# Routed mixture-of-experts kernel: low parts of the weights on VectorE alone while the routing runs, issued one by one; weights of the first expert split during its gather

## The chip, the core and the metric

The kernel runs on one core of a Trainium2 chip. Five engines take part, each with its own queue that is worked off in order: TensorE (PE, the matmuls; PEld is its loading of weights), VectorE (DVE), ScalarE (ACT), GpSimd (POOL) and SyncE (SP), which issues most DMA transfers. The metric is the device time of one execution in microseconds.

## The reference

Three layers follow each other, all in fp32. First comes attention with a local or a strided mask over 4 x 576 tokens, 8 heads of 64 columns; its output is a matrix x of 2304 tokens by 512. Then a routed layer of eight experts, with a greedy assignment by capacity:

```python
logits = x @ w_gate                       # 2304 x 8
order = np.argsort(-logits.flatten())     # best first
# each token goes to one expert, each expert takes cap = 2304 // 8 = 288 tokens
for e in range(8):
    h = np.maximum(x[assigned == e] @ w1[e], 0.0)      # 512 -> 1024
    out[assigned == e] = h @ w2[e]                     # 1024 -> 512
```

Last comes a dense layer of four experts over all tokens, out = sum over e of p[:, e] * (relu(y @ v1[e]) @ v2[e]), where p are given probabilities, each row divided by its sum.

## The kernel before

**Matmuls in three products.** A matmul of the two expert layers is made of three, so that it keeps nearly fp32 accuracy: each operand is split into a high part (a copy rounded to the type fp32r) and a low part (the operand minus its high part), and high x high, low x high and high x low are summed in PSUM. The high part is made by ScalarE. For activations the low part is made by VectorE straight from PSUM (`split`, L804: `xl`, `hl`, `y256l`, `y512l`). For weights the low part `wl` is `raw - wh`, with both inputs in SBUF.

**Units, steps, chunks.** `experts` (L703) runs 20 units: a unit "m1" g is routed expert g for its 288 tokens, a unit "m2" is one dense expert for one to three blocks of 256 or 512 tokens. The routed experts come at units 0, 3, 5, 7, 9, 11, 13, 15, and dense work on tokens already done lies between them. A unit has a step for each eighth of the hidden width and each block. A step is layer one, `l1` (12 matmuls into a PSUM tile `h`), and, two steps later (LK = 2), layer two, `l2` (into tiles `o`); between them the ReLU makes `hh` on ScalarE (L806) and `hl` on VectorE. A chunk is the weights of one eighth: two tiles `raw` of 128 x 512 (256 KB each, one DMA each, L770 and L771 on SP's queue), the high parts `wh` (two copies on ScalarE, L795) and the low parts `wl` (two subtractions, L801). There are 8 buffers for `raw`, which is four chunks, and 8 chunks of `wh` and `wl`.

**What sets the order of the weights' work.** `preps` (L991), called after each `l1`, makes the high parts of a chunk LA = 3 steps ahead of its first use (`prep_hi`, L788), and the low parts one step later (`prep_lo`, L797), both halves of a chunk in one go. `prep_lo` chooses the engine: all lows of odd chunks and the second half of even ones go to GpSimd, the first half of even chunks to VectorE. After the lows of a chunk `loads` (L773) issues the transfers of later chunks; a transfer into a `raw` buffer has to wait until both the high and the low of the chunk that lay in it are done.

**The routing.** Two generators run beside the matmuls. `chain_a` (L814) finds, for each expert, the threshold that lets 288 tokens through: a search in six rounds (`search`), where VectorE compares (`G`), TensorE counts by small matmuls (`pa`, L561), VectorE reduces the counts (`need`, `junk`), TensorE spreads the result (`pa`, L568) and VectorE forms the next thresholds (`d`, `th`, `kb`, `jk`). `chain_b` (L822) turns the found tokens into indices (`place`: `O`, `W`, matmuls L654 and L661, `idx`), gathers their rows by three indirect DMAs on GpSimd (`xg`, L833), transposes them (L850, for the first expert L857) and splits them into `xh` and `xl`. Each generator yields after a piece of work, and says when it wants to go on.

**The planner.** The order is written while the program is built. `Pace` (L676) keeps an estimated clock of TensorE (`nc.pe`, advanced by `mm`, L909, by each large matmul) and one of VectorE (`nc.dve`, advanced by 0.075 us + elements / 960 for each VectorE instruction). `tick` (L895) steps a generator when the time that it asked for (`wake`, L893) is reached. So small matmuls and VectorE work of the routing are put between large matmuls at places that depend on these estimates, and all five engines then work off fixed orders. The engine orders matter because a waiting instruction holds up everything behind it on its engine.

**The start.** When the search for expert 0 is done, L1005 to L1009 issue the loads of chunks 0 to 2, run the chains until the first gather is issued, prepare chunk 0 (`preps(0, 1)`), run on until the gathered rows are split (`x`), and prepare the next chunks. On SP's queue the small transfer `side<-xg` (L837), which waits for the gather, stands between the loads of chunk 2 and of chunk 3.

## Time and profile before

| what | value |
|---|---|
| median of 3 runs | 1290.42 us (1290.1 to 1298.86) |
| the profiled execution, its own time | 1290.25 us |
| its span, first to last instruction | 1288.5 us |
| mean granted TensorE clock | 0.968 |
| PE busy | 1226.5 us (95%) |
| DVE, ACT, POOL busy | 555.8, 417.7, 423.6 us |

The attention fills the time up to about 170 us, with the search for expert 0 at its end. The first routed expert's matmuls begin at 180.2 us. The searches for the other experts run beside the matmuls until shortly before 500 us, the gathers until some 700 us. From 830 us on only dense work is left. All times below are counted from the span's start. A busy PE is not PE at its peak: matmuls overlap, and at a lower granted clock they are longer and still count as busy.

### The profile page before, as it was taken

What the parts mean: (1) busy time and instruction counts of PE and PEld (TensorE: products, weight loads), DVE (VectorE), ACT (ScalarE), POOL (GpSimd) and SP (SyncE); (2) the same over time, 40 slices, a digit from 0 to 9 for tenths busy, and PEclk for the clock granted to TensorE, in tenths of its full rate; (3) what the DMA queues carried; (4) which work ended last, traced back from release to release, by engine and by line L of the source; (5) the groups of instructions that cost most, each with busy time, mean ns of one, the idle gap of its engine ahead of it and who ended that gap; (6) DMA issues with size and microseconds to landing.
All of it is one profiled execution on the core that took longest, in us unless ns stands there. A gap on an engine that the chain in (4) does not pass through costs nothing.

```text
span 1288.5 us, 21205 instructions
## 1 busy us (share of the span) xinstructions
PE 1226.5 (95%) x7883; PEld 1034.2 (80%) x7883; DVE 555.8 (43%) x1618; ACT 417.7 (32%) x1110; POOL 423.6 (33%) x385
## 2 busy tenths in 40 slices
PE   7899859888998999999999999999999999999997
PEld 5676658777877889889888898988888888888886
DVE  4476566978777663233134332422231122123212
ACT  4687543332332234134134252321130131013110
POOL 3133144645244355145155453620050022004101
PEclk7699979999999999999999999999999999999999
DMA  6664274544334345035134353520040021002001
GB/s 136 144 153 87 57 214 123 155 134 121 88 101 116 86 123 157 23 105 155 44 115 123 110 155 93 170 66 1 1 131 1 1 74 57 1 1 66 25 9 50
DMA packets 159767, 114.99 MB, mean 89 GB/s; under 512 B 45104, under 2 KB 136256, under 8 KB 159088
## 3 DMA queue, kind: packets, MB, share of 16 engines
q1 hardware_dynamic: 156592, 104.01, 29.2%
q0 software_dynamic: 3072, 9.62, 2.4%
q8 instruction: 62, 1.02, 0.3%
q14 instruction: 41, 0.34, 0.1%
HBM read 104.02 MB, written 9.58 MB: 88 GB/s over the span
## 4 chain that ended last, share of the span: by engine, by line
PE 81%; DVE 8%; DMA 3%; issue 3%; SPq 2%; ACT 1%; POOL 1%; POOLq 0%; DVEq 0%; ACTq 0%
PE h L910 37%; PE o L910 35%; DVE G L699 2%; DMA ks<-in_k_dram 2%; DVE wl L699 1%; DMA raw<-in_moe_w_dram 1%; PE pt L211 1%; PE pa L561 1%; PE tr L143 1%; SPq L67 1%; SPq L57 1%; PE xr L302 1%; DVE th L699 1%; PE av L224 1%; PE xr L305 1%
## 5 line engine op out<-in xcount | busy, mean ns | idle before, releaser
L801 POOL TENSOR_TENSOR wl<-raw,wh 128x512 fp32r<-128x512 f32 x239 | 336.4, 1424 | 571.8 <-ACT wh L795 481.3
L699 DVE SCALAR_TENSOR_TENSOR hl<-h,hh 128x256 fp32r<-128x256 f32 (+2 forms) x256 | 136.1, 532 | 588.8 <-ACT hh L806 585.5
L806 ACT ACTIVATE hh<-h 128x256 fp32r<-128x256 f32 (+2 forms) x256 | 120.8, 472 | 763.5 <-PE h L910 747.0
L910 PE MATMUL o<-wh,hl 128*128 128x512 f32 x576 | 229.9, 399 | 0.0
L910 PE MATMUL o<-wl,hh 128*128 128x512 f32 x576 | 229.3, 398 | 0.0
L910 PE MATMUL o<-wh,hh 128*128 128x512 f32 x576 | 228.7, 397 | 0.0
L795 ACT CAST wh<-raw 128x512 fp32r<-128x512 f32 x320 | 181.4, 618 | 9.5 <-DMA raw<-in_moe_w_dram 9.4
L910 PE MATMUL h<-hold,wh 128*128 128x512 f32 x384 | 152.4, 397 | 0.0
L910 PE MATMUL h<-y512l,wh 128*128 128x512 f32 x384 | 151.6, 395 | 0.0
L910 PE MATMUL h<-hold,wl 128*128 128x512 f32 x384 | 150.8, 393 | 0.0
L910 PEld LDWEIGHTS o<-wh,hl 128*128 128x128 f32 x576 | 108.7, 189 | 25.2 <-issue 0.3
L910 PEld LDWEIGHTS o<-wl,hh 128*128 128x128 f32 x576 | 108.8, 189 | 21.5
L910 PEld LDWEIGHTS o<-wh,hh 128*128 128x128 f32 x576 | 108.4, 188 | 21.8 <-issue 0.2
L910 PE MATMUL h<-y256h,wh 128*128 128x256 f32 x384 | 110.1, 287 | 0.0
L910 PE MATMUL h<-y256h,wl 128*128 128x256 f32 x384 | 109.9, 286 | 0.0
L910 PE MATMUL h<-y256l,wh 128*128 128x256 f32 x384 | 109.6, 285 | 0.0
L699 DVE TENSOR_TENSOR wl<-raw,wh 128x512 fp32r<-128x512 f32 x81 | 90.0, 1111 | 1.4 <-ACT wh L795 1.4
L910 PEld LDWEIGHTS h<-hold,wl 128*128 128x128 f32 x384 | 72.1, 188 | 17.6
L910 PEld LDWEIGHTS h<-hold,wh 128*128 128x128 f32 x384 | 72.1, 188 | 16.1
L910 PEld LDWEIGHTS h<-y512l,wh 128*128 128x128 f32 x384 | 72.1, 188 | 15.9
L910 PE MATMUL o<-hh,wh 128*128 128x288 f32 x256 | 77.2, 301 | 3.4 <-DVE acc L699 3.4
L910 PE MATMUL h<-xl,wh 128*128 128x288 f32 x256 | 78.9, 308 | 0.0
(221 smaller groups left out, 1838.1 us busy)
## 6 DMA issues: line engine op xcount, KB each, us to landing
raw<-in_moe_w_dram SPq DMA_DIRECT2D x320, 256.0 KB
vl<-in_v_dram SPq DMA_DIRECT2D x32, 96.0 KB
qs<-in_q_dram SPq DMA_DIRECT2D x4, 576.0 KB
ks<-in_k_dram SPq DMA_DIRECT2D x4, 576.0 KB
ql<-in_q_dram SPq DMA_DIRECT2D x16, 144.0 KB
kl<-in_k_dram SPq DMA_DIRECT2D x16, 144.0 KB
xd<-y512l SPq DMA_DIRECT2D x9, 192.0 KB
xd<-y512l SPq DMA_DIRECT2D x2, 576.0 KB
```

What stands on the lines that cost most here:

```text
L57: nc.sync.dma_start(T[nm][:, :, h, :], dap(src, (b * H + h) * hs, [6 * D, 96], [D, 6], [1, D]))
L67: nc.sync.dma_start(T["vs"][18 * p:18 * (p + m), t], dap(v, (b * H + 4 + h) * hs + 2 * rp * D, [2 * D, m], [32 * D, 18], [1, 2 * D]))
L143: nc.tensor.transpose(p[:, 72 * a:72 * a + 72], src[:, r:r + 2, :].rearrange("p r d -> p (r d)"), ident[:72, :72])
L211: nc.tensor.transpose(p[:keys, rows * j:rows * j + rows], T["p"][:rows, j, :keys], ident[:rows, :rows])
L224: nc.tensor.matmul(p[64 * par:64 * par + 64, a, :rows], LD[b]["vs"][:keys, 2 * g + a, 64 * par:64 * par + 64], T["pT"][:keys, rows * j:row ...
L302: nc.tensor.matmul(p[:16, :m], wgs[:, h], XTS[b].rearrange("p h j r -> p h (j r)")[:, h, i0:i0 + m], start=h == 0, stop=False)
L305: nc.tensor.matmul(p[:16, :m], wgl[:, hp, 8 - 8 * par:24 - 8 * par], XTL[b][:, hp, 2 * i0 + par:2 * i0 + 2 * m:2], start=False, stop=par + ...
L699: return f(*args, **kw)
L795: nc.scalar.copy(c["h"][:, sl], c["raw"][a])
L801: (nc.gpsimd if k and (a or k % 2) else nc.vector).tensor_tensor(c["l"][:, sl], c["raw"][a], c["h"].bitcast(FT)[:, sl], OP.subtract)
L806: nc.scalar.activation(hi, src, AF.Relu)
L910: nc.tensor.matmul(out, a, b, start=start, stop=stop)
```

## The change

The numbers and rules of the planner change, and so the order on all engines; the instructions are the same, apart from the engine that makes some `wl`. (1) `prep_lo` becomes `split_lo`, which makes one half of a chunk. While a generator is still alive (`chains` not empty) it always takes VectorE; afterwards the old rule holds. (2) `fill`, called at the end of each `tick`, issues one such half whenever the estimated VectorE clock is not ahead of TensorE's and the chunk's high parts are at least HI = 2.0 us old. What `fill` has not issued, `preps` forces later than before: one step ahead of the chunk's use. (3) LA goes from 3 to 4, so high parts are made a step earlier. (4) At the start the first PRE = 5 chunks are split in full, high and low, before the program goes on to the gathered rows; second halves of chunks 1 to 4 go to GpSimd. (5) The estimates change: 0.15 us instead of 0.075 us for a VectorE instruction, a little more for a matmul (n / 2315 + 0.009), DS from 0.25 to 0.4 and counted from VectorE's clock, PP from 0.15 to 0.25, and a step that only queues VectorE work may be issued 0.8 us ahead. `chain_b` is stepped before `chain_a`.

```diff
-LA = 3
+LA = 4
-AFT, DS, PP, GA = 0.25, 0.25, 0.15, 2.5
+AFT, DS, PP, GA = 0.25, 0.4, 0.25, 2.5
+HI = 2.0
+PRE = 5
...
-            self.dve = max(self.dve, self.pe) + 0.075 + n / 960
+            self.dve = max(self.dve, self.pe) + 0.15 + n / 960
...
-        def prep_lo(k):
+        def split_lo(pool=False):
+            k, a = divmod(state["lo"], 2)
             c = chunks[k]
-            for a in range(2):
-                sl = slice(512 * a, 512 * a + 512)
-                (nc.gpsimd if k and (a or k % 2) else nc.vector).tensor_tensor(c["l"][:, sl], c["raw"][a], c["h"].bitcast(FT)[:, sl], OP.subtract)
-            loads(0, NRAW)
+            sl = slice(512 * a, 512 * a + 512)
+            eng = nc.gpsimd if pool or not chains and (a or k % 2) else nc.vector
+            eng.tensor_tensor(c["l"][:, sl], c["raw"][a], c["h"].bitcast(FT)[:, sl], OP.subtract)
+            state["lo"] += 1
+            if a:
+                loads(0, NRAW)
+
+        def fill():
+            while chains and state["lo"] < 2 * state["prep"] and nc.dve <= nc.pe and chunks[state["lo"] // 2]["at"] + HI <= nc.pe:
+                split_lo()
...
-                wake[n] = {"q": (nc.pe, 0.0), "d": (nc.pe, DS), "p": (nc.pe + PP, None), "idle": (nc.pe + 0.5, None), "hold": (nc.pe + 3.0, None)}.get(d) or (nc.pe + d, None)
+                wake[n] = {"q": (nc.pe, -0.8), "d": (nc.dve + DS, None), "p": (nc.pe + PP, None), "idle": (nc.pe + 0.5, None), "hold": (nc.pe + 3.0, None)}.get(d) or (nc.pe + d, None)
...
-            tick(n / 2400 + 0.0025)
+            tick(n / 2315 + 0.009)
...
-            while state["lo"] < state["prep"] and (chunks[state["lo"]]["prep"] < s or chunks[state["lo"]]["first"] <= s):
-                prep_lo(state["lo"])
-                state["lo"] += 1
+            while state["lo"] < 2 * state["prep"]:
+                c = chunks[state["lo"] // 2]
+                if c["first"] > s + (1 if chains else 0) and (chains or c["prep"] >= s):
+                    break
+                split_lo()
...
-        preps(0, 1)
+        for k in range(PRE):
+            prep_hi(k)
+            state["prep"] += 1
+            for a in range(2):
+                split_lo(a and k)
```

**First place: the start, VectorE and ScalarE.** ScalarE's order before, from the last copy of the attention's output (`hold<-o`) on:

```order
L269 COPY hold<-o 96x256 x6
L795 CAST wh<-raw 128x512 x2
L810 CAST xh<-o 128x288 x4
L795 CAST wh<-raw 128x512 x6
L806 ACTIVATE hh<-h 128x288
```

and ScalarE's order after the change, from the same place:

```order
L269 COPY hold<-o 96x256 x6
L798 CAST wh<-raw 128x512 x10
L822 CAST xh<-o 128x288 x4
L818 ACTIVATE hh<-h 128x288
L798 CAST wh<-raw 128x512 x2
```

The ten high copies of chunks 0 to 4 now stand ahead of the four copies `xh`, for which the first expert's matmuls wait; before it was the two of chunk 0. VectorE's order after the change at the same place, from the positions of the chosen tokens (`pmem`) to the split of the gathered rows (`xl`):

```order
L701 TENSOR_TENSOR pmem<-pos 128x18
L701 TENSOR_SCALAR bm<-pmem 128x18
L701 TENSOR_SCALAR eb<-w_83,esf 128x8
L701 SCALAR_TENSOR_TENSOR L<-bm,L 128x144
L701 TENSOR_SCALAR kj<-pmem 128x18 x2
...
L701 CAST idx<-pb 96x3
L701 SCALAR_TENSOR_TENSOR L<-eb,L 128x144
L701 TENSOR_TENSOR wl<-raw,wh 128x512 x6
L701 TENSOR_TENSOR xl<-o,xh 128x288 x4
```

Six lows instead of two stand ahead of `xl`, and three short instructions (`bm`, `eb`, `L`), which stood behind the lows, stand ahead of `kj` and so of the gather's indices `idx`. The order of SP's queue is the same here: loads of chunks 0 to 2, `side<-xg`, loads of chunk 3 and on.

**Second place: a round of the search for expert 1, VectorE.** Before, from the table `jk` for the third round to the next round's compare:

```order
L699 TENSOR_TENSOR jk<-jsh_119,kb 128x32
L699 SCALAR_TENSOR_TENSOR hl<-h,hh 128x288
L699 TENSOR_TENSOR wl<-raw,wh 128x512
L699 TENSOR_SCALAR need<-pa 8x31
L699 SCALAR_TENSOR_TENSOR junk,sat<-pa,need 8x31
L699 TENSOR_REDUCE d<-pa 128x1
L699 TENSOR_TENSOR th<-jk,d 128x32
L699 TENSOR_TENSOR G<-m_148,th 128x12x32
L699 SCALAR_TENSOR_TENSOR hl<-h,hh 128x288
```

and after the change, the same round:

```order
L701 TENSOR_TENSOR jk<-jsh_119,kb 128x32
L701 TENSOR_TENSOR wl<-raw,wh 128x512
L701 SCALAR_TENSOR_TENSOR hl<-h,hh 128x288
L701 TENSOR_TENSOR wl<-raw,wh 128x512
L701 TENSOR_SCALAR need<-pa 8x31
L701 SCALAR_TENSOR_TENSOR junk,sat<-pa,need 8x31
L701 TENSOR_TENSOR wl<-raw,wh 128x512
L701 TENSOR_REDUCE d<-pa 128x1
L701 TENSOR_TENSOR th<-jk,d 128x32
L701 TENSOR_TENSOR G<-m_148,th 128x12x32
```

Three lows stand singly in the round where there was one, at the points where VectorE waits for TensorE's counts. On GpSimd 4 lows are left between the first and the second gather, where there were 29, and then none until after the last gather.

## Rows read from the trace of the kernel before

**Rows 1.** The page: engine busy time; ScalarE groups: busy us, mean ns, idle

```profile
PE 1226.5 (95%) x7883; PEld 1034.2 (80%) x7883; DVE 555.8 (43%) x1618; ACT 417.7 (32%) x1110; POOL 423.6 (33%) x385
...
L806 ACT ACTIVATE hh<-h 128x256 fp32r<-128x256 f32 (+2 forms) x256 | 120.8, 472 | 763.5 <-PE h L910 747.0
...
L795 ACT CAST wh<-raw 128x512 fp32r<-128x512 f32 x320 | 181.4, 618 | 9.5 <-DMA raw<-in_moe_w_dram 9.4
```

**Rows 2.** Whom PE waited for, 180 to 500 us: total, times, longest

```profile
PE pa L561 <- DVE G L699: 10.4, 13, 2.9
PE pa L568 <- DVE junk L699: 4.3, 4, 3.0
PE o L910 <- DVE acc L699: 3.4, 2, 1.7
PE pb L654 <- DVE W L699: 2.8, 3, 1.7
PE pa L615 <- DVE st L699: 1.5, 1, 1.5
PE pa L616 <- DVE ei L699: 0.5, 2, 0.3
```

**Rows 3.** Busy by stretch: PE, PEld, DVE, ACT, POOL; clock, DMA share, GB/s

```profile
190.00:200.00 10.00, 7.96 (x40) 7.35 (x40) 6.62 (x14) 2.06 (x4) 7.73 (x6) 0.66 0.60 175
...
230.00:240.00 10.00, 10.00 (x55) 8.89 (x55) 9.42 (x18) 4.23 (x9) 5.98 (x5) 0.84 0.45 138
...
260.00:270.00 10.00, 7.65 (x47) 6.73 (x48) 6.02 (x21) 2.84 (x7) 2.84 (x2) 0.83 0.49 148
...
310.00:320.00 10.00, 6.83 (x45) 6.26 (x44) 7.80 (x15) 2.20 (x5) 4.45 (x4) 0.83 0.35 101
...
340.00:370.00 30.00, 29.97 (x230) 25.14 (x229) 20.50 (x70) 5.44 (x13) 5.71 (x6) 1.00 0.12 30
...
180.00:500.00 320.00, 296.78 (x2161) 261.35 (x2160) 231.93 (x628) 112.40 (x255) 157.62 (x118) 0.96 0.43 124
...
560.00:760.00 200.00, 199.33 (x1194) 176.49 (x1193) 67.29 (x122) 70.51 (x151) 94.26 (x72) 1.00 0.39 115
```

**Rows 4.** DVE groups, 170 to 750 us: count, busy us, mean ns, idle

```profile
L699 DVE TENSOR_TENSOR wl<-raw,wh 128x512 fp32r<-128x512 f32 x57 | 54.2, 951 | 1.4 <-ACT wh L795 1.4
...
L699 DVE SCALAR_TENSOR_TENSOR hl<-h,hh 128x288 fp32r<-128x288 f32 x53 | 24.1, 455 | 71.2 <-ACT hh L806 71.1
...
L699 DVE TENSOR_TENSOR th<-jk,d 128x32 int32<-128x32 int32 x24 | 11.5, 479 | 0.8
```

**Rows 5.** GpSimd's groups by form, 150 to 750 us, columns as in rows 4

```profile
L801 POOL TENSOR_TENSOR wl<-raw,wh 128x512 fp32r<-128x512 f32 x168 | 236.6, 1424 | 243.2 <-ACT wh L795 181.7 <-PE o L910 18.8 <-issue 12.4
L833 POOL DMA_INDIRECT xg<-xd,idx x24 | 23.6, 985 | 90.3 <-DMA raw<-in_moe_w_dram 30.8 <-DVE idx L699 29.6 <-DVE m L699 20.2
```

**Rows 6.** All engines in time around the first gather: start, length in us

```profile
163.97 0.19 DVE L699 TENSOR_TENSOR th<-jk,d 128x32 int32<-128x32 int32 x1
...
172.49 1.40 DVE L699 TENSOR_TENSOR wl<-raw,wh 128x512 fp32r<-128x512 f32 x2 [1.38 <-ACT wh L795]
...
174.01 0.30 DVE L699 SCALAR_TENSOR_TENSOR L<-bm,L 128x144 f32<-128x144 f32 x1
...
179.08 0.33 SPq L837 DMA_DIRECT2D side<-xg  x1
...
180.21 0.61 PE L910 MATMUL h<-xh,wh 128*128 128x288 f32 x1
```

**Rows 7.** The chain that ended last, 140 to 520 us: start us, length us

```profile
181.81 4.67 DMA raw<-in_moe_w_dram
...
255.87 2.44 DMA raw<-in_moe_w_dram
...
284.54 5.21 DMA raw<-in_moe_w_dram
...
304.94 1.60 PE o L910 x12
```

More of the change, by code (lines that the diff above doesn't have):

```diff
@@ L790, in prep_hi @@
             c = chunks[k]
+            c["at"] = nc.pe
             c["h"] = mp.tile([128, 1024], FR, name="wh", bufs=NSLOT)
@@ L877, in more @@
                     deferred.pop(0)(lambda: ps.tile([128, 512], FT, name="o", bufs=4), keep, nc.scalar.copy)
-        chains = {"a": chain_a(), "b": chain_b()}
+        chains = {"b": chain_b(), "a": chain_a()}
         wake = {"a": (0.0, None), "b": (0.0, None)}
@@ L902, in tick @@
                     step(n)
+            fill()
         def until(f):
```

## The prediction

> **What bounds the kernel now.** I read the page first, then the busy time by stretch, then whom TensorE waited for, and last the rows of single instructions. TensorE is busy for 95% of the span [rows 1], so only a stretch in which it stands still, or works at a low granted clock, has something to give. Such a stretch is the one in which the searches run: from 180 to 500 us TensorE was busy for 296.78 of 320 us [rows 3]. Its waits there name VectorE each time: 10.4 for `G`, 4.3 for `junk`, 3.4 for an `o` tile, 2.8 for `W`, 1.5 for `st`, 0.5 for `ei`, together 22.9 us [rows 2]. After a long wait the granted clock falls to the lower level for some microseconds: it was 0.66 from 190 to 200, 0.84 from 230 to 240, 0.83 from 260 to 270 and 0.83 from 310 to 320 us [rows 3]. Against full speed that is 3.4 + 1.6 + 1.7 + 1.7 = 8.4 us. I count it as 8, since a part of the first lies in idle time that is in the waits already. So 31 us of this stretch are not work.
>
> Why VectorE is late is seen in its own rows. `th`, 32 elements with both inputs in SBUF, took 0.19 us when GpSimd had no low in hand [rows 6], and 0.479 on the mean over the routing [rows 4]. The low of a weight took 1.40 us for two, 0.70 each, during the gather [rows 6], and 0.951 on the mean [rows 4]. `hl`, which reads PSUM, is not drawn out in this way (mean 0.455 [rows 4]). In this stretch GpSimd makes most lows at 1.424 us each [rows 5] and was busy for 157.62 us [rows 3]. So a VectorE instruction with two SBUF inputs seems to wait for the end of GpSimd's low, and the search is a chain of just such instructions. The best row for it is the stretch from 340 to 370 us: the search goes on there (230 matmuls, 70 VectorE instructions), GpSimd was busy for only 5.71 of 30 us, and TensorE stood still for 0.03 us at a granted clock of 1.00 [rows 3].
>
> **The change part by part.** *Lows to VectorE (a gain).* Between 180 and 500 us GpSimd's 157.62 us hold at most 157.62 / 1.424 = 110 lows. On VectorE they cost 110 x 0.70 = 77 us. It gets back what it now loses by waiting: 57 x (0.951 - 0.70) = 14 us at its own lows and 24 x (0.479 - 0.19) = 7 us at `th` (counts from [rows 4]). About ten other forms with two SBUF inputs have no price here of their own; I put them between nothing and the same 21 us again, and take 21, since `th` shows that a short instruction loses as much as a long one. The load goes from 231.93 us to 232 + 77 - 42 = 267 us, of a stretch that should become about 300 us long: 89%, and 96% if the other forms give nothing. That is an upper bound of the load, since the order puts the searches of the last experts later, past 500 us, into a stretch with more room. The gain is bounded by 31 us above and by nothing below.
>
> *What stays of the waits.* At a VectorE share of 20.50 / 30 = 68% TensorE did not wait [rows 3]; the new share is higher. On the other hand the lows come one at a time, 0.70 us is the most that one can hold up the search, and the planner's price for a low (0.15 + 512 / 960 = 0.683 us) is now close to the row. I take a fifth of the 31 us, 6 us, as staying, between 0 (the stretch from 340 on) and 31.
>
> *The start (a loss).* Before, the first expert's first matmul began at 180.21 us, as soon as the first `xh` stood [rows 6]. Now ten high copies stand ahead of `xh`, so ScalarE has to wait for the loads of chunk 4. These cannot come early: they stand on SP's queue behind `side<-xg`, which went out at 179.08 us [rows 6], and the last of them was issued at 181.81 and landed 4.67 us later, at 186.48 [rows 7]. Its high copy is 0.618 us [rows 1], so `xh` starts at about 187.1, and its first copy of 288 columns takes some 0.35 us (an estimate, 288 / 512 of that). Besides, three short VectorE instructions now stand ahead of `idx`, of which `L` takes 0.30 us [rows 6]; with at most that for each of the others the gather goes out 0.7 us later (0.9 at most), and all behind it. The first matmul moves from 180.2 to about 188.2 us: 8 us lost. Bounds: 6 us if the load lands in the 2.44 us of another row, 9 us if it takes 5.21 [rows 7]. What is won for it is not counted twice: with five chunks split, the waits at 190 us, which are in the 31 us, have no cause left.
>
> One rule speaks against this place. The gather's three issues took 0.985 us each on the mean [rows 5], while VectorE made two lows beside them [rows 6]. The Trainium skill, in "SBUF — State Buffer", section "SBUF: two separate sides", says that VectorE and GpSimd share one pair of ports, that whichever starts first holds it for the whole instruction, and that descriptors of a DMA issued by GpSimd can be starved by this. By it each of the three issues could wait for one of the six lows, 3 x 0.70 = 2 us more at the start, and the sum below would be 1275 instead of 1273 us. The rows do not ask for it, since 0.985 us is the mean over all eight gathers, most of them with VectorE at work; I leave it out.
>
> *The rest, at nothing.* LA = 4 only makes high copies a step earlier; ScalarE is idle for most of the stretch (112.40 of 320 us busy [rows 3]), and if that cover were gone each chunk would cost two copies, 1.24 us [rows 1]. The number of small matmuls is the same, so what they cost between large ones cancels. Past 500 us TensorE has next to nothing to win (199.33 of 200 us busy from 560 on), and GpSimd's lows there go to a VectorE with room (67.29 of 200 us busy) until the last gather [rows 3]. The search moved past 500 us costs there what it cost before 500.
>
> **Sum**, against the profiled execution's own time: 1290.25 - 22.9 - 8 + 8 + 6 = 1273 us. That execution is 0.2 us below the median of the runs, so the forecast for the median is the same.
>
> **The rivals.** *VectorE gets full.* At 89 to 96% of the stretch the search may queue behind lows that `preps` forces. Then half of the 31 us stay: 1290.25 - 31 + 8 + 15.5 = 1283 us. For it: the bound above. Against it: the bound leaves out the move past 500 us, and 68% gave no wait at all.
>
> *The waits are not the lock's.* If TensorE waits because a small matmul simply stands too early in its order, nothing is won but by the new DS and PP, and the start is lost: 1290.25 + 8 = 1298 us at worst. Against it: the same search without GpSimd's lows had no waits [rows 3].
>
> *The raw buffers come back late (slower).* Lows are now made up to the last step but one, and the load of the chunk four places on waits for them. In the order its high copy stands one step behind that low, on ScalarE between two ReLUs. The loop is: a low 0.70, the landing, a high copy 0.618, a ReLU 0.472 [rows 1], `hl` 0.455 [rows 4], the next low 0.70, so 2.95 us and the landing, over two steps. Half a step of a routed expert is 12 matmuls in 1.60 us [rows 7], so two steps are 6.4 us, and the loop decides from a landing of about 3.5 us on. One row has 2.44, two have 4.67 and 5.21 [rows 7], the latter two issued close behind other loads. At 5.21 two steps take 8.2 us, 0.9 us more for each of the 56 steps of units 0 to 3, 5 and 7 and of the first blocks of 4 and 6 (8 each, 64 less the first 8): 1290.25 - 31 + 8 + 50 = 1317 us; at a landing of 4.67 it is 0.6 us, so 1301 us. Against it: in the single row where a load was issued alone it took 2.44, and the ReLU has two steps until layer two needs it.
>
> **How the numbers follow.** Likeliest case 0.53, 1273 us, its own range 1266 to 1279; VectorE full 0.26, about 1283; no lock 0.09, 1290 to 1298; buffers late 0.12, 1301 to 1317. A difference of about 1% (13 us) is what a measurement of this kernel can tell from none. Faster than that needs less than 1277.5 us: most of the likeliest case and a little of the second, 0.52. Slower needs more than 1303: most of the last, 0.11. The rest, 0.37, is within 1%. For 8 in 10 the range goes from 1265 to 1291: it leaves out the last case, most of the third and a little of the first.
>
> **What would show it.** Lows on VectorE near 0.70 us and `th` near 0.19 in the routing; TensorE's waits for `G`, `junk` and `W` under 6 us between 180 and 500; the granted clock 1.00 there but for the start; the first matmul of expert 0 near 188 us. The forecast is wrong if ScalarE waits for `raw` by more than a few microseconds after 200 us (the third rival), if VectorE is busy for over 90% and TensorE still waits (the first), or if `th` is short and TensorE waits all the same (the second).

## The result and the profile after

The changed kernel takes 1269.61 us (median of 4 runs, 1269.19 to 1270.36), the kernel before, in runs beside it, 1292.3 us. The ratio of the runs is 0.9826, with a 95% interval of [0.9801, 0.9851]: faster by 1.7%. The forecast was 1273 us with a range of 1265 to 1291. The later comparisons had the kernel before at 1293.5, 1294.6 and 1294.8 us, so experiments are compared by ratio.

Three lines of the page of the changed kernel: the span, the busy time of each engine, and the granted clock in 40 slices (tenths):

```profile
span 1267.9 us, 20941 instructions
...
PE 1216.4 (96%) x7881; PEld 1023.8 (81%) x7883; DVE 585.6 (46%) x1793; ACT 425.4 (34%) x1110; POOL 178.1 (14%) x210
...
PEclk9698969999999999999999999999999999999999
```

TensorE was busy for 10 us less in all (1226.5 before [rows 1]), and GpSimd's 423.6 us became 178.1. Whom TensorE waited for from 180 to 500 us (total, times, longest), against [rows 2]:

```profile
PE h L923 <- ACT xh L822: 7.0, 1, 7.0
PE pb L862 <- DVE xl L701: 3.8, 4, 1.9
PE o L923 <- DVE y512l L701: 1.8, 2, 0.9
PE h L923 <- DVE y256l L701: 0.4, 1, 0.4
```

`G`, `junk`, `acc`, `W`, `st` and `ei` are gone altogether. The first row is the start; the other three, 6.0 us together, are new kinds of wait. The same stretches as in [rows 3] (PE, PEld, DVE, ACT, POOL busy; clock, DMA share, GB/s):

```profile
190.00:200.00 10.00, 10.00 (x75) 9.55 (x74) 5.98 (x19) 5.72 (x12) 0.00 (x0) 0.94 0.45 125
230.00:240.00 10.00, 10.00 (x73) 8.38 (x72) 8.33 (x30) 5.92 (x11) 0.00 (x0) 1.00 0.52 168
260.00:270.00 10.00, 7.73 (x52) 6.66 (x51) 6.55 (x14) 5.18 (x11) 0.00 (x0) 1.00 0.50 149
310.00:320.00 10.00, 10.00 (x67) 8.94 (x66) 6.69 (x24) 1.15 (x3) 0.00 (x0) 1.00 0.20 64
...
180.00:500.00 320.00, 306.83 (x2255) 271.79 (x2255) 224.98 (x676) 127.11 (x275) 17.50 (x19) 0.98 0.43 130
```

The granted clock is 1.00 where it was 0.83 and 0.84. TensorE gains 10 us of busy time in the 320. VectorE, with over a hundred more lows in this stretch, is busy for 224.98 us against 231.93. Part of that is work moved out of the stretch (one search now lies past 500 us): over the whole execution VectorE's busy time rose, from 555.8 to 585.6 us. The rows behind that are its groups and GpSimd's (count, busy us, mean ns, idle), against [rows 4, 5]:

```profile
L701 DVE TENSOR_TENSOR wl<-raw,wh 128x512 fp32r<-128x512 f32 x232 | 151.8, 687 | 10.9 <-ACT wh L798 9.8
...
L701 DVE SCALAR_TENSOR_TENSOR hl<-h,hh 128x288 fp32r<-128x288 f32 x56 | 25.6, 457 | 53.6 <-ACT hh L818 53.6
...
L701 DVE TENSOR_TENSOR th<-jk,d 128x32 int32<-128x32 int32 x24 | 4.6, 192 | 0.8
```

```profile
L845 POOL DMA_INDIRECT xg<-xd,idx x24 | 24.7, 1030 | 475.0 <-DVE idx L701 388.3 <-DVE mw L701 50.6 <-DMA raw<-in_moe_w_dram 31.2
L806 POOL TENSOR_TENSOR wl<-raw,wh 128x512 fp32r<-128x512 f32 x4 | 5.5, 1379 | 5.9 <-ACT wh L798 5.9
```

`th` fell from 479 to 192 ns, a low on VectorE from 951 to 687 ns; `hl`, which reads PSUM, stayed (455 and 457). The means of the kernel before mix two kinds of instruction, as single rows of it show (start, length, idle time before):

```profile
254.09 4.28 DVE L699 TENSOR_TENSOR jk<-jsh,kb 128x32 int32<-128x32 int32 x1
254.53 5.13 POOL L801 TENSOR_TENSOR wl<-raw,wh 128x512 fp32r<-128x512 f32 x4
...
262.35 0.18 PE L568 MATMUL pa<-id,sat 8*128 8x8 bf16 x1 [2.97 <-DVE junk L699]
...
416.42 1.28 POOL L801 TENSOR_TENSOR wl<-raw,wh 128x512 fp32r<-128x512 f32 x1 [2.87 <-PE pa L568]
416.63 1.12 DVE L699 TENSOR_TENSOR th<-jk,d 128x32 int32<-128x32 int32 x1
```

Of the 24 `th` before, 18 took 0.19 us. The other six began while GpSimd was at work and took 0.28 to 4.36 us; the one shown ends 0.05 us after GpSimd's low. All 17 lows on VectorE that took over 0.70 us (of 57) end 0.55 us after a low of GpSimd. `jk` at 254.09 began during the issue of the second gather, behind which four lows of GpSimd had queued; it went through three of them before it ended, and TensorE's longest wait for `junk`, 2.97 us, follows in the same search. So a VectorE instruction that comes second waits until GpSimd has finished, and sometimes for several in a row.

The start in order of time, against [rows 6, 7]:

```profile
180.03 0.33 SPq L849 DMA_DIRECT2D side<-xg  x1
...
182.76 0.34 SPq L773 DMA_DIRECT2D raw<-in_moe_w_dram  x1
...
186.33 1.29 ACT L798 CAST wh<-raw 128x512 fp32r<-128x512 f32 x2 [1.29 <-DMA raw<-in_moe_w_dram]
...
187.53 1.29 ACT L822 CAST xh<-o 128x288 fp32r<-128x288 f32 x4
...
187.97 0.61 PE L923 MATMUL h<-xh,wh 128*128 128x288 f32 x1 [7.03 <-ACT xh L822]
```

The first matmul comes at 187.97 us, 7.8 us later than before. Of that 1.1 us had gone by before anything changed: executions differ in how long the attention takes, and `pmem`, the first instruction after the search for expert 0, came at 167.92 us before and at 169.02 here (166.28 to 169.99 over all profiled runs). Counted from `pmem`, the first matmul is 6.7 us later (18.95 against 12.28 us). The load issued at 182.76 is that of chunk 4; its high copies end as the first `xh` begins.

### The profile page after: what moved, and what is told of

It reads as the page before. It is cut to its first block, busy times and chain, and to the rows that moved or that the text cites. A ratio compares the mean times of both kernels' runs of the same rounds, so it can differ in the third digit from the quotient of the medians.

```text
span 1267.9 us, 20941 instructions
## 1 busy us (share of the span) xinstructions
PE 1216.4 (96%) x7881; PEld 1023.8 (81%) x7883; DVE 585.6 (46%) x1793; ACT 425.4 (34%) x1110; POOL 178.1 (14%) x210
## 3 DMA queue, kind: packets, MB, share of 16 engines
q1 hardware_dynamic: 156592, 104.01, 28.9%
q8 instruction: 62, 1.02, 0.3%
HBM read 104.02 MB, written 9.58 MB: 90 GB/s over the span
## 4 chain that ended last, share of the span: by engine, by line
PE 87%; DMA 4%; DVE 4%; issue 2%; ACT 1%; SPq 1%; POOL 1%; DVEq 0%; POOLq 0%; ACTq 0%
PE h L923 39%; PE o L923 38%; DMA ks<-in_k_dram 2%; DMA raw<-in_moe_w_dram 2%; PE tr L143 1%; PE pa L561 1%; PE pt L211 1%; PE xr L302 1%; PE av L224 1%; DVE wl L701 1%; PE xr L305 1%; PE s L175 1%; PE tr L153 1%; PE s L178 1%; PE pb L862 0%
## 5 line engine op out<-in xcount | busy, mean ns | idle before, releaser
L798 ACT CAST wh<-raw 128x512 fp32r<-128x512 f32 x320 | 185.8, 618 | 51.8 <-DMA raw<-in_moe_w_dram 50.6
L701 DVE TENSOR_TENSOR wl<-raw,wh 128x512 fp32r<-128x512 f32 x256 | 179.2, 730 | 10.9 <-ACT wh L798 9.8
L806 POOL TENSOR_TENSOR wl<-raw,wh 128x512 fp32r<-128x512 f32 x64 | 89.8, 1419 | 378.7 <-ACT wh L798 368.0
L845 POOL DMA_INDIRECT xg<-xd,idx x24 | 24.7, 1030 | 475.0 <-DVE idx L701 388.3
L923 PE MATMUL h<-xh,wh 128*128 128x288 f32 x256 | 76.5, 299 | 7.0 <-ACT xh L822 7.0
```

The lines of the kernel that those rows point to most:

```text
L701: return f(*args, **kw)
L798: nc.scalar.copy(c["h"][:, sl], c["raw"][a])
L806: eng.tensor_tensor(c["l"][:, sl], c["raw"][a], c["h"].bitcast(FT)[:, sl], OP.subtract)
L845: nc.gpsimd.indirect_dma_start(out=xg[:, k, :], out_offset=None, in_=xd, in_offset=bass.IndirectOffsetOnAxis(ap=idx[:, k:k + 1], axis=0))
L923: nc.tensor.matmul(out, a, b, start=start, stop=stop)
```

## The experiments

The change puts two things together: lows off GpSimd, and another order. So the first question was which of them carries the gain; then what the start and the raw buffers cost; then which part of the order counts. Every ratio is to the kernel before in runs on the same chip. The times in the last column are from one profiled run each, and carry the shift of up to 3.7 us in `pmem`.

| kernel | median us | ratio, 95% interval | second gather issued at us |
|---|---|---|---|
| before | 1292.3 to 1294.8 | 1 | 250.92 |
| changed | 1269.61 | 0.9826 [0.9801, 0.9851] | 249.07 |
| e1 before, lows on VectorE | 1277.24 | 0.9889 [0.9855, 0.9922] | 271.27 |
| e2 changed, lows on GpSimd | 1292.0 | 0.9995 [0.9976, 1.0013] | 237.76 |
| e3 changed, old start | 1272.01 | 0.9855 [0.9822, 0.9889] | 255.36 |
| e4 changed, `side` later | 1266.3 | 0.9813 [0.9776, 0.985] | 243.08 |
| e5 changed, old planner numbers | 1276.79 | 0.9864 [0.9848, 0.988] | 274.40 |
| e6 changed, ten raw buffers | 1266.59 | 0.9781 [0.9765, 0.9796] | 248.84 |
| e7 changed, GpSimd subtracts too | 1323.81 | 1.0236 [1.0217, 1.0255] | 257.64 |
| e8 changed, `side` later, ten raw | 1262.59 | 0.9759 [0.9745, 0.9772] | 245.51 |
| e9 changed, old prices | 1265.93 | 0.9786 [0.9753, 0.9818] | 239.90 |
| e10 changed, old waking | 1281.91 | 0.9901 [0.9881, 0.9921] | 275.87 |
| e11 changed, lows in pairs | 1278.98 | 0.9883 [0.9859, 0.9907] | 261.78 |
| e12 changed, GpSimd copies too | 1274.69 | 0.9848 [0.9828, 0.9868] | 249.10 |

**e1: the engine alone.** The kernel before, its rules of order untouched:

```diff
-(nc.gpsimd if k and (a or k % 2) else nc.vector).tensor_tensor(
+(nc.gpsimd if not chains and (a or k % 2) else nc.vector).tensor_tensor(
```

> The kernel before with one edit: while a generator of the routing is alive, all lows of weights are made by VectorE, still two at a time and at the old places and old planner's prices. Theory of the lock (a VectorE instruction with two SBUF inputs waits for GpSimd's low): th near 0.19 us and a low near 0.70 us; TensorE's waits between 180 and 500 us fall from 22.9 to 10 to 15 us, since the lows come in pairs and at unplanned moments; time about 1279 us. Rival (the places in the order make the waits): th is short as well, but TensorE's waits stay at 20 us or more, time 1288 us or above.

Measured: 1277.24 us. `th` is 192 ns on the mean and the low 682 ns, as in the changed kernel. TensorE's waits from 180 to 500 us:

```profile
PE o L857 <- DMA xg<-xd,idx: 8.0, 1, 8.0
PE pa L561 <- DVE G L699: 6.9, 8, 2.1
PE pb L654 <- DVE W L699: 4.0, 2, 3.8
PE pa L568 <- DVE junk L699: 4.0, 6, 1.4
```

The first row is the start. Waits for `G`, `W` and `junk` are still there, 14.9 us of them (17.5 before [rows 2]), nearly all of them between 240 and 300 us; all waits but the start's come to 17.9 us, more than the 10 to 15 expected. The time, 1279 expected, is the lock theory's. So taking the lows off GpSimd is worth 1.1%, some 14 of the 22 us, without any new rule of order; but with the old rules the second expert's search comes late (its gather at 271.27 us, 20 us later than before).

**e2: the order alone.** The changed kernel with the old choice of engine:

```diff
-            eng = nc.gpsimd if pool or not chains and (a or k % 2) else nc.vector
+            eng = nc.gpsimd if pool or k and (a or k % 2) else nc.vector
```

> The changed kernel with one edit: the old rule for the engine (odd chunks and second halves to GpSimd) holds during the routing too; all planner's numbers, the single issue and the start stay. Theory of the lock: th back to 0.4 us or more, a low on VectorE back to 0.9, TensorE's waits for G, junk and W back to 10 us or more between 200 and 500 us, time about 1284 us. Rival (the new places alone bring the gain, VectorE has even less to do here): TensorE's waits stay near 6 us, time 1270 us or below.

Measured: 0.9995, nothing. TensorE's waits, and VectorE's groups from 170 to 750 us:

```profile
PE pa L561 <- DVE G L701: 17.4, 8, 8.6
```

```profile
L701 DVE TENSOR_TENSOR wl<-raw,wh 128x512 fp32r<-128x512 f32 x58 | 68.8, 1187 | 8.8 <-ACT wh L798 8.1
...
L701 DVE TENSOR_TENSOR th<-jk,d 128x32 int32<-128x32 int32 x24 | 10.3, 429 | 0.8
```

The long times are back (`th` 429 ns, the low 1187 ns) and so are the waits for `G`, 17.4 us. The longest of them, 8.6 us, follows these two rows:

```profile
241.68 12.09 DVE L701 TENSOR_TENSOR wl<-raw,wh 128x512 fp32r<-128x512 f32 x1
242.09 11.13 POOL L806 TENSOR_TENSOR wl<-raw,wh 128x512 fp32r<-128x512 f32 x9
```

A single low on VectorE, begun during the issue of the second gather, lasted until the nine lows that GpSimd had queued behind that issue were through; the search stood behind it. The time is 8 us above the 1284 expected. The new order without the change of engine gains nothing, with the later start in it (first matmul at 188.04 us); what the order is worth without that start was not run.

**e7: GpSimd's subtraction beside VectorE's, for nobody.** e1 and e2 leave open whether GpSimd's lows cost by holding VectorE up or by being long themselves (1.42 us), so that a matmul waits for them. Here all lows that are used come from VectorE; GpSimd makes the same subtraction into a spare tile.

```diff
             eng.tensor_tensor(c["l"][:, sl], c["raw"][a], c["h"].bitcast(FT)[:, sl], OP.subtract)
+            if eng is nc.vector and chains and k and (a or k % 2):
+                nc.gpsimd.tensor_tensor(mp.tile([128, 512], FR, name="spare", bufs=2), c["raw"][a], c["h"].bitcast(FT)[:, sl], OP.subtract)
```

> The changed kernel, in which GpSimd makes while the routing runs, beside each low that it would have had before, the same subtraction of raw and wh into a spare tile that nobody reads. Every low that TensorE uses still comes from VectorE, so no matmul waits for GpSimd's 1.4 us. Theory A (the lock alone: GpSimd's subtraction stretches VectorE's instructions with two inputs in SBUF): th goes from 0.192 us back above 0.40, wl on VectorE from 0.687 to 0.85 or more; VectorE's busy time from 180 to 500 rises from 225 us to over 290 (232 lows at 0.27 more are 62 us), it becomes the bound, and the time is 1295 us or more. Rival B (the long lows on GpSimd came late, the stretch did not matter): th and wl as in the changed kernel, or longer without effect, and 1268 to 1273.

Measured: 1323.81 us, slower than before by 2.4%.

```profile
L701 DVE TENSOR_TENSOR wl<-raw,wh 128x512 fp32r<-128x512 f32 x209 | 219.1, 1079 | 8.2 <-ACT wh L798 7.4
...
L701 DVE TENSOR_TENSOR th<-jk,d 128x32 int32<-128x32 int32 x24 | 10.1, 419 | 0.8
```

```profile
L808 POOL TENSOR_TENSOR spare<-raw,wh 128x512 fp32r<-128x512 f32 x155 | 228.1, 1488 | 195.8 <-ACT wh L798 178.7 <-DMA raw<-in_moe_w_dram 9.6 <-issue 5.5
```

`th` is back at 419 ns and a low takes 1079 ns, though VectorE's program is that of the changed kernel and no result of GpSimd's is waited for. Between 170 and 750 us, 209 lows at 0.392 us more on the mean are 82 us of VectorE. From 180 to 500 us it was busy for 269.74 us (I had expected over 290: fewer of its instructions fell into the stretch), and TensorE's waits behind VectorE rose from 6.0 to 35.8 us. The spare reads also hold raw buffers longer (ScalarE waited 81.9 us for `raw`, in the changed kernel 41.4), so not all of the 54 us is VectorE's; that `th` and `wl` are drawn out by GpSimd's work is shown by it.

**e12: one input in place of two.** The same places, but GpSimd copies `wh` into the spare tile:

```diff
+                nc.gpsimd.tensor_copy(mp.tile([128, 512], FR, name="spare", bufs=2), c["h"].bitcast(FT)[:, sl])
```

> The changed kernel in which GpSimd, at the places where it made a spare subtraction of raw and wh before (1323.8 us, th 0.419 us, wl 1.079 us), makes a plain copy of wh into the spare tile instead: one input in SBUF and not two, nobody reads it. Theory A (any GpSimd instruction that reads and writes SBUF stretches VectorE's two-input ones while it runs): th above 0.3 us, wl above 0.85 us, 1290 us or more. Theory B (only GpSimd's two-input form holds VectorE up): th within 0.19 to 0.21 us, wl 0.69 to 0.72 us, and 1268 to 1275 us; a gain over the changed kernel isn't to be had by it.

Measured: 1274.69 us, between the two theories.

```profile
L701 DVE TENSOR_TENSOR wl<-raw,wh 128x512 fp32r<-128x512 f32 x232 | 171.1, 770 | 9.7 <-ACT wh L798 8.5
...
L701 DVE TENSOR_TENSOR th<-jk,d 128x32 int32<-128x32 int32 x24 | 6.4, 268 | 0.8
```

```profile
L808 POOL CAST spare<-wh 128x512 fp32r<-128x512 f32 x172 | 141.1, 837 | 278.9 <-ACT wh L798 278.5 <-POOL spare L808 0.2
```

A copy takes 837 ns, and with 172 of them the mean of `th` is 268 and that of the low 770 ns. So an instruction of GpSimd with one input holds VectorE up as well: 232 x 0.083 = 19 us on lows for 141 us of GpSimd, against 82 us for 228 us in e7. Neither theory's numbers hold, but the single rows decide between their mechanisms:

```profile
355.39 0.62 POOL L808 CAST spare<-wh 128x512 fp32r<-128x512 f32 x1 [2.69 <-ACT wh L798]
355.40 0.65 DVE L701 TENSOR_TENSOR th<-jk,d 128x32 int32<-128x32 int32 x1
```

Of 24 `th`, 18 took 0.19 us here too, and the six others end 0.04 us after a copy, as those in e7 end 0.05 us after a subtraction. The hold is the same, to the end of GpSimd's instruction; a copy alone is only shorter (0.62 us, a subtraction 1.29). That is theory A with too high a price. The time is 5 us longer than the changed kernel's by the median, but the intervals of the two ratios overlap.

**e3: the start put back.** The changed kernel with one chunk prepared ahead of the gathered rows, as before:

```diff
-        for k in range(PRE):
-            prep_hi(k)
...
+        preps(0, 1)
```

> The changed kernel with the old start: only chunk 0 is split before the gathered rows, the others behind them. If the start is a plain loss of 8 us, as the sum of the prediction has it: first matmul of expert 0 near 181 us, no long wait behind it, time about 1262 us. Rival (what is lost at the start is won again in the first expert, whose weights would otherwise come late): waits of 2 us or more and a low granted clock between 185 and 200 us come back, time 1269 us or above.

Measured: 0.9855, and in the profiled runs 1267.5 us of span against 1267.9. The first matmul comes at 178.85 us, 9.1 us ahead of the changed kernel's (6.7 us counted from `pmem`), and nothing of that is left at the end. Where it went (columns as in [rows 3]):

```profile
190.00:200.00 10.00, 9.58 (x75) 9.02 (x74) 6.81 (x17) 5.77 (x12) 0.00 (x0) 1.00 0.58 183
...
260.00:270.00 10.00, 4.81 (x33) 3.23 (x31) 8.44 (x23) 2.33 (x5) 0.00 (x0) 0.71 0.55 166
310.00:320.00 10.00, 7.73 (x54) 6.60 (x52) 7.24 (x25) 5.08 (x16) 0.00 (x0) 1.00 0.39 122
```

From 260 to 270 us TensorE is busy for 4.81 us at a clock of 0.71, in the changed kernel for 7.73 us at 1.00; it waits there for `G`, `junk` and `xl`, that is for the second expert's search and split. That expert's gather goes out at 255.36 us, 6 us later than in the changed kernel, though TensorE started 9 us sooner. The early split does not make the kernel measurably faster or slower, then (the intervals overlap); it goes with a wait at the start in place of one at 260 us. Why the second search is later without it was not followed.

**e4: the side table written later.** `side<-xg` of the first expert goes out behind its split, as for the other experts, and no longer stands on SP's queue ahead of the loads of chunk 3 and 4:

```diff
-                if g == 0:
-                    nc.sync.dma_start(dap(side, 0, [8, 96], [96 * 8, 3], [1, 8]), xg[:, :, 512:])
...
-                if g:
+                if True:
                     nc.sync.dma_start(dap(side, 8 * CAP * g, [8, 96], [96 * 8, 3], [1, 8]), xg[:, :, 512:])
```

> The changed kernel with the small transfer side<-xg of expert 0 issued after the gathered rows are split, as for the other experts, so that the loads of chunks 3 and on no longer stand behind the gather on SP's queue. If that queue order is what makes the first matmul late: chunk 4 has landed before the gather, first matmul of expert 0 near 181 us with all five chunks split, time about 1262 us. Rival (the gather shares the transfer engines with the loads and lands later): the transposes begin at 182 us or later, first matmul at 185 us or later, time 1267 us or above.

Measured: 1266.3 us; the intervals of this ratio and the changed kernel's overlap. In the profiled runs the span is 1262.2 us against 1267.9, and the whole difference is there at the first matmul:

```profile
181.26 0.90 PE L868 MATMUL o<-ident,xg 96*128 96x96 f32 x4 [0.65 <-DMA xg<-xd,idx]
182.17 0.61 PE L922 MATMUL h<-xh,wh 128*128 128x288 f32 x1
```

The first matmul is at 182.17 in place of 187.97 us. But `pmem` came at 166.28 us here and at 169.02 in the changed kernel, in the same instructions: 2.7 us of the 5.8 are not this edit's. Counted from `pmem` the first matmul is 3.1 us sooner (15.89 against 18.95 us), and still 3.6 us later than before (12.28). The wait for `xh` is gone, and what ends the start now is the gather: its third part reaches TensorE at 181.26, 10.4 us after its first issue, where it was 6.5 us in the changed kernel. So theory and rival both came true in part: the queue behind `side<-xg` made the start late, and with the loads let past it the gather lands late beside them.

**e6 and e8: ten raw buffers.** In the changed kernel ScalarE waits for raw weights (total, times, longest, from 180 to 570 us), and these waits were named ahead as a sign of a slower kernel:

```profile
ACT wh L798 <- DMA raw<-in_moe_w_dram: 41.4, 44, 5.0
```

```diff
-NRAW = 4
+NRAW = 5
```

> The changed kernel with ten raw buffers in place of eight, and the loads issued five chunks ahead in place of four. ScalarE waited 41.4 us for raw (44 times) in the changed kernel between 180 and 570 us. Theory A (these waits lie off the chain that sets the time, since the wh copies stand several chunks ahead of their matmuls): ScalarE's waits for raw fall below 20 us, TensorE's waits in 180 to 500 stay at 10 to 14 us with the start's 7, and the time stays within 3 us of the changed kernel's 1269.6. Rival B (late raw weights are what keeps the rest of TensorE's waits and the xl waits alive): 1263 to 1266.

Measured: 0.9781 [0.9765, 0.9796], which lies below the changed kernel's interval. The wait fell to

```profile
ACT wh L798 <- DMA raw<-in_moe_w_dram: 5.4, 3, 4.5
```

and TensorE's waits for `xl` from 3.8 to 1.3 us. The way from the one to the other is seen in the changed kernel (start, length, idle time before):

```profile
261.24 0.62 ACT L798 CAST wh<-raw 128x512 fp32r<-128x512 f32 x1 [1.84 <-DMA raw<-in_moe_w_dram]
...
262.48 0.62 ACT L798 CAST wh<-raw 128x512 fp32r<-128x512 f32 x1 [0.62 <-DMA raw<-in_moe_w_dram]
263.01 0.39 ACT L822 CAST xh<-pb 128x288 fp32r<-128x288 f32 x1
...
263.44 0.46 DVE L701 TENSOR_TENSOR xl<-pb,xh 128x288 fp32r<-128x288 f32 x1 [1.43 <-ACT xh L822]
...
263.95 0.47 PE L862 MATMUL pb<-ident,xg 96*128 96x96 f32 x3 [1.89 <-DVE xl L701]
```

ScalarE stands still for 1.84 and 0.62 us for raw weights, the `xh` of the next expert's rows is queued behind these copies, `xl` behind `xh`, and the transpose that needs the PSUM tile waits 1.89 us. So 36 us of ScalarE's waits are worth some 4 us of the kernel (spans 1267.9 and 1263.7, of which 0.6 us by the first matmul). By the median, 1266.59 us, neither theory's numbers decide; by the trace it is more than nothing, which theory A called it, and far less than the prediction's third rival had it. With the side table moved too:

> The changed kernel with both small changes: the side table of the first expert written after its x, not before it, and ten raw buffers. The first alone gave 1266.3 us (the first matmul at 182.2 in place of 188.0 and all after it 5.8 us earlier in the profiled run). Theory A (late raw weights cost nothing): 1263 to 1268, as with the first alone. Rival B (they cost): 1259 to 1262.

Measured: 1262.59 us, 0.9759 [0.9745, 0.9772]. This is the fastest version, 2.4% under the kernel before and 7 us under the changed kernel's median. The time lies between the two theories' ranges. The gains of e4 and e6 do not quite add up: the spans would give 1258, and it is 1260.4. Counted from `pmem` they nearly do, 2.9 and 3.8 us against 5.8 together.

**e5, e9, e10: which of the planner's numbers.** First all of them put back, with the lows on VectorE and issued singly:

```diff
-AFT, DS, PP, GA = 0.25, 0.4, 0.25, 2.5
+AFT, DS, PP, GA = 0.25, 0.25, 0.15, 2.5
-            self.dve = max(self.dve, self.pe) + 0.15 + n / 960
+            self.dve = max(self.dve, self.pe) + 0.075 + n / 960
-        chains = {"b": chain_b(), "a": chain_a()}
+        chains = {"a": chain_a(), "b": chain_b()}
-  "q": (nc.pe, -0.8), "d": (nc.dve + DS, None)
+  "q": (nc.pe, 0.0), "d": (nc.pe, DS)
-            tick(n / 2315 + 0.009)
+            tick(n / 2400 + 0.0025)
```

> The changed kernel with the planner's numbers, the wake rule and the order of the two routing chains put back to those of before (matmul price, VectorE price, DS, PP, the two rules of waking); the lows stay on VectorE, issued singly in the planner's idle time, and the start stays changed. Theory A (the single issue needs only VectorE's place in the planner, the numbers are fine tuning): 1268 to 1275 us, TensorE's waits from 180 to 500 us under 15 us. Rival B (the numbers are what makes VectorE's idle time come out right): near the run that only changed the lows' engine, 1277 us or more, with waits for G, junk and W back above 12 us in 180 to 500.

Measured: 1276.79 us, no better than e1 (the intervals overlap), with 14.2 us of waits for `G`, `junk` and `tk`. Without the new numbers, then, the single issue and the changed start together add nothing to e1's gain. Then the two prices alone (`0.075` and `n / 2400 + 0.0025`):

> The changed kernel with only the planner's two prices put back (a VectorE instruction 0.075 us plus its elements, a matmul n/2400 + 0.0025): the planner's picture of VectorE's idle time is the only thing that differs. All numbers, rules and orders put back together gave 1276.8 us, 24 us over the bare matmuls in the second full expert (about 239 to 291 us). Theory A (the prices are what matters: with VectorE priced too low, lows are issued into time that isn't idle and the routing's search falls behind): 1275 to 1278 us, and waits for G, junk or tk of 10 us or more in 180 to 500. Theory B (the rules of waking and the chain order matter): 1268 to 1271, waits of that kind under 3 us.

Measured: 0.9786 [0.9753, 0.9818]: theory A fell. Old prices cost nothing; the run is rather faster than the changed kernel (the intervals overlap, so I leave that open), and it has no wait for `G` or `junk`. Then the rest, the rules of waking with DS and PP and the order of the chains:

> The changed kernel with only the rules of waking (q, d, DS, PP) and the order of the two routing chains put back, the new prices kept. Theory A (prices): 1268 to 1271 us and waits for G, junk and tk under 3 us in 180 to 500. Theory B (waking and order): 1275 to 1278 us, with such waits of 10 us or more.

Measured: 1281.91 us, 12 us slower than the changed kernel by the median and some 10 by the ratio. TensorE's waits:

```profile
PE pa L568 <- DVE junk L701: 6.6, 7, 2.2
PE pa L561 <- DVE G L701: 6.0, 5, 2.2
PE pb L661 <- DVE tk L701: 3.9, 1, 3.9
```

The second gather goes out at 275.87 us, 27 us later than in the changed kernel, though the first matmul, at 185.8 us, is 2 us earlier. The code says why. By the old rule a step of the search that needs VectorE is woken only once the planner's clock of VectorE is DS behind TensorE's; but `fill` issues a low as soon as the two are level, and each low pushes VectorE's clock ahead again. The search is put off for as long as there are lows. By the new rule the time of waking is fixed when the step before is issued, and no later low moves it. The runs fit this: the old rule with lows on VectorE gave 271, 274 and 276 us for the second gather (e1, where pairs of lows push the clock, as there is no `fill`, e5 and e10), the new one 237 to 262 in all others, and with lows on GpSimd, which the planner doesn't price, the old rule did no harm (250.92). What DS, PP and the order of the chains do by themselves was not tried, so the 12 us belong to all of them together.

**e11: lows in pairs.** The changed kernel without `fill`, so that `preps` makes both lows of a chunk at its due step:

```diff
-            fill()
```

> The changed kernel without the rule that issues one low whenever the planner's VectorE is idle: each low is made at its due step, two of a chunk in a row as before, all on VectorE; prices, waking and start stay changed. Theory A (single issue in idle time is a real part of the gain: 2 x 0.687 us ahead of the routing's short instructions delay them): waits for G, junk and W above 10 us in 180 to 500, 1275 to 1280 us. Rival B (the engine and the planner's numbers are all): 1268 to 1271 us, such waits under 3 us.

Measured: 0.9883 [0.9859, 0.9907], 9 us slower by the median and 7 by the ratio, but not by the waits that theory A named: `G` and `junk` are 2.8 us. ScalarE's wait for raw weights is

```profile
ACT wh L798 <- DMA raw<-in_moe_w_dram: 61.7, 62, 4.7
```

and the second gather is 13 us later than in the changed kernel, which fits lows that are made at the last step and give their raw buffers back late. That `fill` is worth 7 to 9 us is shown. Whether that comes of issuing lows singly or of issuing them before the last step is not: the edit takes away both. TensorE's waits without the start, 9.1 us against 6.0, make a third of it, and the lower mean clock (0.96 against 0.98 of 320 us, about 6 us, by rounded means) most of the rest; which of the late buffers and the late search does more is open.

## Why the prediction was right

**The mechanism was right, and it is the larger part.** `th` fell to 192 ns and the low to 687 ns as forecast, and e1, e2 and e7 tie that to GpSimd's work. "Waits for the end of GpSimd's low" is borne out row by row; what the prediction did not see is that it can be several lows in a row. The two longest waits of TensorE before, 2.97 us for `junk` and 2.87 us for `G`, come behind a `jk` of 4.28 and a `th` of 4.36 us, each held by three. The Trainium skill, in "SBUF — State Buffer", section "Who interferes with whom", says that a VectorE instruction with two SBUF inputs contends with a GpSimd instruction that reads SBUF. The traces agree (`th` 479 ns beside GpSimd's lows, 192 without), and so does e12's copy, which reads one tile (`th` at 268 ns).

**The sum, term by term.** The spans differ by 20.6 us (1288.5 and 1267.9). TensorE's waits went from 22.9 to 6.0 us, 16.9 less; the forecast had 22.9 less and 6 back, the same. The start cost 7.8 us against 8, of which 6.7 are the change's. That leaves 11.5 us (20.6 - 16.9 + 7.8) for the term of the low granted clock, which was put at 8. By the mean clock of the stretch (0.96 and 0.98 of 320 us) about 6 us of it are the clock (the means are rounded, so 3 to 10); the rest I can't assign. The total was off by 3.4 us, the size of this term's error, and the time lies in the likeliest case's own range, 1266 to 1279.

**What stayed was not what I said would stay.** The 6 us were to be searches that queue behind lows on a fuller VectorE. Instead they are `xl`, `y512l` and `y256l`, and e6 shows most of the first to come from raw weights that land late (3.8 us, with ten buffers 1.3). That the numbers agree is chance.

**VectorE's load was put too high: 267 us, measured 225.** The lows were sized well: 136 in place of 33 from 180 to 500 us, 60.0 us more (28.9 to 88.9), where 77 less 14 had been reckoned for 110 (the 14 took the 57 lows of 170 to 750 us for those of this stretch, which are 33). But all else on VectorE fell from 203.0 to 136.1 us, where 28 us had been allowed. Nearly every form with two inputs in SBUF had been drawn out, not `th` and a few: on the mean the 192-column `G` took 765 ns before and 351 after, `jk` 360 and 191, `kb` 330 and 152. So had `kj`, with one input (322 and 171). Summed over the stretch, instruction by instruction against the same form's median after, this excess was some 53 of the 67 us. The rest goes with work moved past 500 us, one of the six searches among it. So the first rival, VectorE full, was given too much (0.26).

**The start was right in size and wrong in its use.** Its chain came as described: `side<-xg`, the loads behind it, ten copies, `xh`. e4 confirms the queue as the cause of what was lost, but frees only 3.1 of the 6.7 us, since the gather then lands later. And the prediction booked it as a net loss of 8 us, and e3 shows that without it the time is the same: the loss is paid at 260 us instead. The reason given for not counting a gain, that the waits at 190 us have no cause left with five chunks split, is wrong too: in e3 the stretch from 190 to 200 us runs at 9.58 us busy and a clock of 1.00 without them.

**The sign of the third rival came, its price didn't.** ScalarE waited 41.4 us for raw weights, and I had written that the forecast is wrong if that happens. The loop was reckoned as if each late landing held TensorE up for its whole excess, 34 us and more. e6 puts it at some 4 us: high copies stand steps ahead of their matmuls, and only where an `xh` is queued behind one does it show. The sign should have been a wait of TensorE for `hl` or `xl`.

**The order was priced at nothing but was a condition.** The rules of waking with DS, PP and the chains' order are worth 10 to 12 us (e10) and `fill` 7 to 9 us (e11). The sum took the whole gain from GpSimd's leaving VectorE alone and left the planner's numbers out; it came out right because these numbers do keep the search on time once VectorE's clock carries the lows. e1 is near what the change would have been without them: a gain of 1.1% in place of 1.7%.

**The rule that was weighed was rightly left out.** The gather's three issues took 1.02 + 1.32 + 0.92 = 3.26 us before and 1.46 + 0.95 + 0.92 = 3.33 us after, with two and three lows on VectorE beside them: no starving that costs 2 us. But the price is not nothing: with no two-input VectorE instruction beside it an issue takes 0.92 to 0.95 us, and the changed kernel's with two lows beside them took 1.46 and, for the last gather, 1.76. It cancels here because the kernel before had lows beside its issues too. The rule as the Trainium skill has it, in "SBUF — State Buffer", section "SBUF: two separate sides", ties the starving to a VectorE instruction in a two-port mode, a condition that the prediction left out.

## What to carry to other kernels

Where the same instruction has two lengths in one trace, look which other engine works beside it, and price it by both: a mean hides the few long ones on which the others wait. Moving work to the other engine can then cost that engine much less than the work's length. When work moves to an engine that a planner keeps a clock for, look at each rule that waits for that clock: the moved work can starve what the move was meant to help. A wait of an engine that runs ahead is no price by itself: follow it to what is queued behind the waiting instruction. And before a start is compared between two profiled runs, count it from the last instruction that both have in common.

## What the runs showed of the hardware

GpSimd's instruction need not be waited for by anyone to cost time: beside 155 subtractions of 1488 ns, 209 lows on VectorE were 392 ns longer on the mean, and beside 172 copies of 837 ns, 232 lows were 83 ns longer. The shortest suffer with the long ones: `kb`, one element in each partition, took 152 ns in the changed kernel and 332 ns in e7.

The one that comes second waits for the end of the other. In the kernel before, in e2, e7 and e12 each `th` of over 0.20 us ended 0.04 to 0.06 us after an instruction of GpSimd. The hold goes both ways: a low on GpSimd took 1.29 us alone and 1.60 to 1.69 us when it began behind a low on VectorE (kernel before). Where several of GpSimd's stand in a row, a VectorE instruction got in after the first in some rows (a low of 1.08 us at 184.89 us in the kernel before) and not in others: it waited through three lows for 4.36 us in the kernel before, and through nine for 12.09 us in e2. These two began during a gather's issue; what decides is open.
